# A chunk's attention scores as one product per head, with the level-by-level path kept behind a branch

## The chip, the cores and the metric

The kernel runs on one core of one Trainium2 chip. Its engines work side by side and meet at semaphores: TensorE (PE; its weight loads are listed apart as PEld), VectorE (DVE), ScalarE (ACT), GpSimd (POOL) and SyncE (SP). TensorE takes its operands from SBUF and leaves its results in PSUM, from where DVE or ACT fetch them. In this kernel SP and ACT issue the DMAs. The metric is the time of one execution on the device in microseconds; the less, the better.

## The reference

An RWKV-5 attention block (4 batches, 8 heads, 768 tokens, 48 channels a head) is followed by a feed-forward block with a softmax linear unit (3072 tokens, 384 to 1024 to 384):

```python
for t in range(S):
    kt, vt, rt = (k[:, :, t], v[:, :, t], r[:, :, t])
    cur = np.einsum('bhd,bhe->bhde', u[None] * kt, vt)
    y[:, :, t] = np.einsum('bhd,bhde->bhe', rt, state + cur)
    state = w[None, :, :, None] * state + np.einsum('bhd,bhe->bhde', kt, vt)
...
h = x @ w_in
e = np.exp(h - np.max(h, axis=-1, keepdims=True))
solu = h * (e / (np.sum(e, axis=-1, keepdims=True) + 1e-09))
mu, var = solu.mean(-1, keepdims=True), solu.var(-1, keepdims=True)
ln = (solu - mu) / np.sqrt(var + 1e-06) * g_ln
return ln @ w_out
```

The inputs are random. w, the decay of each channel, lies between 0.85 and 0.95. The two weight matrices arrive as float64; all arithmetic is float32.

## The kernel before

**Units.** The 768 tokens of a batch are cut into 6 chunks of 128 tokens. A unit is one chunk of one batch; there are 24, chunk by chunk with the four batches inside, so that a batch's next chunk comes four units after the one whose state it needs.

**Scores.** Inside a chunk, token s reaches a later token t with the weight w^(t-1-s). The kernel splits the 128 by 128 triangle into seven levels L = 64, 32, ..., 1: a pair (s, t) belongs to the level whose block of 2L tokens has s in its lower half and t in its upper half. For each level but the last, `prepare` multiplies the transposed k on POOL (L231) and the transposed r on DVE (L233) with powers of w whose exponents are never negative; the results are the tiles `z`. `scores` multiplies the halves on TensorE, 8 heads a level (L266), and brings them from PSUM into the score matrix `AT`: levels 64 and 32 by copies on ACT (L279), the other five by predicated copies on DVE (L274). `AT` is set to zero once, at the start. The token itself, weighted by u, goes another way: `rku` = k * u * r on POOL (L245, L246), its sum `own` per head on DVE (L248), and `yd` = v * own on POOL (L250), which is added to y.

**y and the state.** `finish` computes y = rs @ state + AT @ v on TensorE (L290, L295), where `rs` is r times powers of w (DVE, L237), adds `yd` on DVE (L299), and updates the state: k times powers (`kp`, POOL, L240) with v on TensorE (L304), the old state times w^128 on POOL (L307), the sum on DVE (L313).

**Feed-forward.** `ffn_in` transposes x, multiplies with w_in (`h_ps`, L328), and then runs a chain in which each step needs the one before: maximum of h (DVE, L332), exp with its sum (ACT, L334), one over the sum (DVE, L336), the product `solu` with its sum (DVE, L338), the square with its sum (ACT, L342), the variance and its power -1/2 (POOL, L343 and L345), the normalisation of `solu` (DVE, L346). `ffn_out` transposes the result (`t_ps`, L357), copies it out of PSUM (`lnT`, half on DVE and half on ACT), and multiplies with w_out (`o_ps`, L364).

**The loop.** Pass i loads unit i+2, prepares unit i+1, and writes `ffn_in(i-3)`, `scores(i)`, `ffn_out(i-3)`, `finish(i)` in this order. In the first three passes the float64 weights are turned into float32, 14 pieces with seven DVE operations and one or two POOL operations each (L128 to L145). A scheduler then orders the instructions of each engine. Within an engine that order is fixed. Operands carry the buffer's number where the rows further down show one.

Of the kernel before, what the change touches and what calls it, by code (L numbers as in the profile page):

```python
# [9 lines left out]
F32 = mybir.dt.float32  # L10
U32 = mybir.dt.uint32
ACT = mybir.ActivationFunctionType
ALU = mybir.AluOpType
AX = mybir.AxisListType
PSUM = bass.MemoryType.PSUM


@with_exitstack
def kernel(
    ctx: ExitStack,  # L20
    tc: tile.TileContext,
    r: bass.AP,
# [6 lines left out]
    moe_g_ln: bass.AP,  # L29
    out: bass.AP,  # L30
):
    """The recurrence runs in chunks of T = 128 tokens.  Within a chunk token s reaches a later
    token t with the weight w^(t-1-s).  The pair belongs to the one level L (64, 32, ..., 1) whose
    blocks of 2L tokens have s in the lower and t in the upper half; with m the first token of the
    upper half, w^(t-1-s) = w^(t-m) * w^(m-1-s), and neither exponent is ever negative: no w can
    make a factor overflow or be divided by.  A state carries the tokens of the chunks before.

    moe_w_in and moe_w_out come as the words of float64 and are rounded to float32 here; the
    arithmetic is float32 throughout."""
    nc = tc.nc  # L40
    B, H, S, D = r.shape
    T = 128
    P = 64
    C = S // T
    HP = H // 2
    dm = H * D
    dff = moe_w_in.shape[1]
    KD = dm // 128
    KF = dff // 128
    NX = 512  # L50
    LAG = 3
# [3 lines left out]
    const = ctx.enter_context(tc.tile_pool(name="const", bufs=1))  # L55
    apool = ctx.enter_context(tc.tile_pool(name="apool", bufs=2))
    zpool = ctx.enter_context(tc.tile_pool(name="zpool", bufs=2))
    fpool = ctx.enter_context(tc.tile_pool(name="fpool", bufs=2))
    wpool = ctx.enter_context(tc.tile_pool(name="wpool", bufs=2))
    small = ctx.enter_context(tc.tile_pool(name="small", bufs=4))  # L60
    psA = ctx.enter_context(tc.tile_pool(name="psA", bufs=3, space=PSUM))
    psH = ctx.enter_context(tc.tile_pool(name="psH", bufs=1, space=PSUM))
    psM = ctx.enter_context(tc.tile_pool(name="psM", bufs=3, space=PSUM))

    ctx.enter_context(nc.allow_non_contiguous_dma(reason="rows of w and g to the partitions"))

    # chunk-major, so that a batch's next chunk comes B units after the one it waits for
    units = [(b, c) for c in range(C) for b in range(B)]

# [1 line left out]
    NLD = 4  # L71
    rpads = [const.tile([128, H, P], F32, name=f"rpad{i}") for i in range(NLD)]
    kpads = [const.tile([128, H, P], F32, name=f"kpad{i}") for i in range(NLD)]
# [8 lines left out]
            nc.sync.dma_start(out=t[i % NLD][:, :, 0:D],  # L82
                              in_=src[b, :, ts(c, T), :].rearrange("h s d -> s h d"))

# [1 line left out]
    wd = const.tile([128, HP, 1], F32, name="wd")  # L86
    u_bc = const.tile([128, H, D], F32, name="u_bc")
    g_sb = const.tile([128, KF], F32, name="g_sb")
# [9 lines left out]
    load(1)  # L98
    nc.scalar.dma_start(out=g_sb, in_=moe_g_ln.rearrange("(c p) -> p c", p=128))

# [1 line left out]
    def words(x):  # L102
        n, m = x.shape
        t = bass.DRamTensorHandle(x.tensor.name, (n, 2 * m), U32)
# [13 lines left out]
    def convert(j):  # L118
        dst, _, f = pieces[j]
        n = dst.shape[1]  # L120
        raw = raws.pop(j)
        lo, hi = raw[:, :, 0], raw[:, :, 1]
        bias = (1023 - 127) << 20
        ex = wpool.tile([128, n], U32, tag="ex", name="ex")
        ma = wpool.tile([128, n], U32, tag="ma", name="ma")
        low = wpool.tile([128, n], F32, tag="low", name="low")
        # the sign and the exponent, 0 when it lies below float32's: +-2^e
        nc.vector.tensor_single_scalar(out=ex, in_=hi, scalar=0x7FF00000, op=ALU.bitwise_and)  # L128
        nc.vector.tensor_scalar(out=ex, in0=ex, scalar1=float(bias),
                                scalar2=float(bias + (255 << 20)), op0=ALU.max, op1=ALU.min)  # L130
        nc.vector.tensor_scalar(out=ex, in0=ex, scalar1=float(bias), scalar2=8.0,
                                op0=ALU.subtract, op1=ALU.mult)
        nc.vector.scalar_tensor_tensor(out=ex, in0=hi, scalar=0x80000000, in1=ex,
                                       op0=ALU.bitwise_and, op1=ALU.bitwise_or)
        # with the first 20 bits of the fraction, and what the other 32 add
        nc.vector.tensor_scalar(out=ma, in0=hi, scalar1=3, scalar2=0x007FFFF8,
                                op0=ALU.logical_shift_left, op1=ALU.bitwise_and)
        nc.vector.tensor_tensor(out=ma, in0=ma, in1=ex, op=ALU.bitwise_or)
        nc.vector.scalar_tensor_tensor(out=low, in0=lo, scalar=2.0 ** -52, in1=ex.bitcast(F32),
                                       op0=ALU.mult, op1=ALU.mult)  # L140
        if f is None:
            nc.gpsimd.tensor_add(dst, ma.bitcast(F32), low)
        else:
            nc.gpsimd.tensor_add(low, ma.bitcast(F32), low)
            nc.gpsimd.tensor_scalar(out=dst, in0=low, scalar1=g_sb[:, f : f + 1], scalar2=1.0,  # L145
                                    op0=ALU.mult, op1=ALU.mult)
# [6 lines left out]
    neg_half = const.tile([128, 1], F32, name="neg_half")  # L153
    nc.vector.memset(neg_half, -0.5)

    # tab[.., n] = w^n and rev[.., n] = w^(T-1-n), channels on the partitions (two heads a column)
    tab = const.tile([128, HP, T], F32, name="tab")
    rev = const.tile([128, HP, T], F32, name="rev")
    pw = const.tile([128, 8, HP, 1], F32, name="pw")
# [7 lines left out]
        nc.vector.tensor_mul(rev[:, :, T - 2 * n : T - n], rev[:, :, T - n : T], step)  # L167
        nc.vector.tensor_mul(pw[:, j + 1], pw[:, j], pw[:, j])

    # w^(T-1-s) with the tokens on the partitions  # L170
    kdec = const.tile([128, HP, 128], F32, name="kdec")
    kd_ps = psM.tile([128, HP, 128], F32, tag="m", name="kd_ps")
    for a in range(HP):
        nc.tensor.transpose(kd_ps[:, a, :], rev[:, a, :], ident)
    nc.vector.tensor_copy(out=kdec, in_=kd_ps)

    # masks[L][s, j, n] = token s lies in the lower half of the j-th block of 2L
    masks = {}
    for L in MASKED:
        nb = 64 // L  # L180
# [7 lines left out]
        nc.vector.tensor_copy(out=mi[:, 0, :], in_=mf.rearrange("p j n -> p (j n)"))  # L188
        masks[L] = mi

    # AT[s, h, t]: only s < t is ever written, the rest stays zero
    NAT = 2
    ATs = [const.tile([128, H, T], F32, name=f"AT{i}") for i in range(NAT)]
    for t in ATs:
        nc.gpsimd.memset(t, 0.0)
    # the state of each batch, two heads to a block diagonal
    states = [const.tile([128, HP, 2, D], F32, name=f"state{b}") for b in range(B)]
    for t in states:
        nc.vector.memset(t, 0.0)
# [7 lines left out]
        x = t.rearrange("p a (j o n) -> p a j o n", o=2, n=L)  # L207
        return x[:, :, :, 0, :], x[:, :, :, 1, :]

# [1 line left out]
    def prepare(i):  # L211
        b, c = units[i]
        kt, rt, vt = kpads[i % NLD], rpads[i % NLD], vts[i % NLD]
        X = live[i] = {}
        kT = apool.tile([128, HP, T], F32, name="kT")
        rT = apool.tile([128, HP, T], F32, name="rT")
        for src, dst in ((kt, kT), (rt, rT)):
            ps = psM.tile([128, HP, T], F32, tag="m", name="tr_ps")
            for a in range(HP):
                nc.tensor.transpose(ps[:, a, :], pair(src, a), ident)  # L220
            nc.scalar.copy(out=dst, in_=ps)  # L221
        X["kT"], X["rT"] = kT, rT
        X["z"] = {}
        for ls in LEVELS:
            for L in ls:
                if L == 1:
                    continue
                z = X["z"][L] = zpool.tile([128, HP, T], F32, name=f"z{L}")
                shape = [128, HP, 64 // L, L]
                (k_lo, _), (_, r_up), (z_lo, z_up) = halves(kT, L), halves(rT, L), halves(z, L)  # L230
                nc.gpsimd.tensor_mul(z_lo, k_lo,  # L231
                                     rev[:, :, T - L : T].unsqueeze(2).to_broadcast(shape))
                nc.vector.tensor_mul(z_up, r_up,  # L233
                                     tab[:, :, 0:L].unsqueeze(2).to_broadcast(shape))
        if c > 0:
            X["rs"] = apool.tile([128, HP, T], F32, name="rs")
            nc.vector.tensor_mul(X["rs"], rT, tab)  # L237
        if c < C - 1:
            X["kp"] = apool.tile([128, H, P], F32, name="kp")
            nc.gpsimd.tensor_mul(X["kp"].rearrange("p h d -> p (h d)"),  # L240
                                 kt.rearrange("p h d -> p (h d)"),
                                 kdec.rearrange("p a d -> p (a d)"))
        # the token itself, weighted by u
        rku = apool.tile([128, H, D], F32, name="rku")
        nc.gpsimd.tensor_mul(rku, kt[:, :, 0:D], u_bc)  # L245
        nc.gpsimd.tensor_mul(rku, rku, rt[:, :, 0:D])  # L246
        own = small.tile([128, H, 1], F32, name="own")
        nc.vector.tensor_reduce(out=own[:, :, 0], in_=rku, axis=AX.X, op=ALU.add)  # L248
        X["yd"] = apool.tile([128, H, D], F32, name="yd")
        nc.gpsimd.tensor_mul(X["yd"], vt, own.to_broadcast([128, H, D]))  # L250

# [1 line left out]
    def scores(i):  # L253
        X = live[i]
        AT = X["AT"] = ATs[i % NAT]
# [22 lines left out]
                            rows = slice(2 * L * j, 2 * L * j + L)  # L278
                            nc.scalar.copy(out=dst[rows, :, j, :], in_=src[rows, :, j, :])  # L279

# [1 line left out]
    def finish(i):  # L282
        b, c = units[i]
        X = live[i]
# [29 lines left out]
                else:  # L314
                    nc.vector.tensor_copy(out=St[rows, :, q, :], in_=kv_ps[rows, :, q, :])

# [1 line left out]
    def ffn_in(i):  # L318
        X = live[i]
        xt_ps = psM.tile([128, KD, 128], F32, tag="m", name="xt_ps")  # L320
# [25 lines left out]
        nc.vector.tensor_scalar(out=solu, in0=solu, scalar1=nmu, scalar2=rstd,  # L346
                                op0=ALU.add, op1=ALU.mult)

# [1 line left out]
    def ffn_out(i):  # L350
        b, c = units[i]
        X = live.pop(i)
# [40 lines left out]
            finish(i)  # L393


# [1 line left out]
_INS = ['r', 'k', 'v', 'w', 'u', 'moe_w_in', 'moe_w_out', 'moe_g_ln']  # L397
_OUTS = [((3072, 384), 'float32')]
# [25 lines left out]
```

## Time and profile before

| What | Value |
|---|---|
| Time, median of 3 runs | 907.26 us (906.92 to 908.93) |
| The profiled execution: its span | 905.3 us, 1.96 below that median |
| TensorE busy | 784.0 us (87% of the span) |
| its weight loads | 601.0 us (66%) |
| DVE busy | 448.1 us (49%) |
| ACT busy | 158.8 us (18%) |
| POOL busy | 285.0 us (31%) |
| Score matmuls L266, busy together | 341.5 us (272.6 + 68.9) |

The span runs from the first to the last instruction; the timed runs hold a little more than it. A matmul in float32 shows as two records, a transpose as one. Matmuls are pipelined, so the busy time of TensorE is a share of the span in which some matmul was under way, not a measure of how full the array was. "Idle before" with an arrow names the operation whose end let the engine go on.

### The profile page before, as it was taken

Reading aid. Unit: us, or ns where it says so; the run is one execution under the profiler, and the core shown is the slowest. Engines: PE = TensorE matmul, PEld = TensorE weight load, DVE = VectorE, ACT = ScalarE, POOL = GpSimd, SP = SyncE. Lnnn points to the kernel's source line nnn. Section 1 sums busy time; section 2 is a strip of 40 time slices with the busy share of each in tenths; the row PEclk is TensorE's granted clock in tenths of the full one; section 3 lists DMA queues with packets and bytes.
Section 4 is the critical chain, followed back from the end, with each engine's and each line's share of the span. In section 5 each row is a group of like instructions: output and inputs, shape, how many; then the busy total and the mean of one; then the engine's idle time right before and its main releaser. Section 6 shows DMA issues by size and latency. Waiting matters only on the chain.

```text
span 905.3 us, 11284 instructions
## 1 busy us (share of the span) xinstructions
PE 784.0 (87%) x4524; PEld 601.0 (66%) x4524; DVE 448.1 (49%) x826; ACT 158.8 (18%) x361; POOL 285.0 (31%) x345
## 2 busy tenths in 40 slices
PE   1564979999999999999999999999999999998665
PEld 1553977677677677677677677777777677766332
DVE  6969767336346346346346346346346435613111
ACT  1101102121121121121121121121122122111111
POOL 5937544404404404404314314314313212200000
PEclk9555557868868868868868868868869876887877
DMA  9413101101101101101101101101100000000000
GB/s 244 79 53 79 27 1 27 35 1 36 35 1 35 36 1 36 35 1 35 35 1 36 35 1 35 35 1 36 35 1 18 18 10 1 10 9 9 9 9 9
DMA packets 82003, 26.09 MB, mean 29 GB/s; under 512 B 76960, under 2 KB 80160, under 8 KB 81952
## 3 DMA queue, kind: packets, MB, share of 16 engines
q1 hardware_dynamic: 78336, 18.88, 10.1%
q10 hardware_dynamic: 3616, 6.49, 2.4%
q8 instruction: 36, 0.59, 0.2%
q14 instruction: 15, 0.12, 0.0%
HBM read 20.65 MB, written 4.72 MB: 28 GB/s over the span
## 4 chain that ended last, share of the span: by engine, by line
PE 64%; POOL 15%; DVE 15%; issue 2%; DMA 2%; ACT 1%; POOLq 0%; ACTq 0%; DVEq 0%
PE at L266 24%; PE o_ps L364 19%; POOL z L231 7%; PE h_ps L328 6%; PE y_ps L295 5%; PE t_ps L357 5%; DVE AT L274 3%; DVE st L332 2%; POOL rku L245 2%; DVE z L233 2%; PE y_ps L290 2%; POOL kp L240 2%; POOL rku L246 2%; POOL yd L250 1%; PE kv_ps L304 1%
## 5 line engine op out<-in xcount | busy, mean ns | idle before, releaser
L266 PE MATMUL at<-z 48*128 48x64 f32 (+1 forms) x2304 | 272.6, 336 | 67.7 <-DVE AT L274 58.7
L266 PEld LDWEIGHTS at<-z 48*128 48x128 f32 (+1 forms) x2304 | 252.4, 242 | 103.7 <-issue 90.3
L364 PE MATMUL o_ps<-w_out_sb,lnT 128*128 128x384 f32 x384 | 175.4, 624 | 0.0
L364 PEld LDWEIGHTS o_ps<-w_out_sb,lnT 128*128 128x128 f32 x384 | 93.7, 252 | 70.6 <-issue 40.6
L299 DVE TENSOR_TENSOR x<-y_ps,yd 128x384 f32<-128x384 f32 x24 | 13.4, 557 | 243.9 <-PE y_ps L295 243.9
L274 DVE COPY_PREDICATED AT<-mask,at 128x256 f32<-128x256 uint32 x240 | 120.2, 549 | 23.9 <-PE at L266 21.5
L328 PE MATMUL h_ps<-w_in_sb,xT 128*128 128x512 f32 x288 | 130.0, 601 | 1.9 <-ACT xT L324 1.8
L233 DVE TENSOR_TENSOR z<-rT,tab 128x256 f32<-128x256 f32 x144 | 114.0, 856 | 17.9 <-ACT rT L221 17.9
L231 POOL TENSOR_TENSOR z<-kT,rev 128x256 f32<-128x256 f32 x144 | 119.8, 863 | 1.2 <-ACT kT L221 1.2
L328 PEld LDWEIGHTS h_ps<-w_in_sb,xT 128*128 128x128 f32 x288 | 52.7, 190 | 61.5 <-issue 57.4
L343 POOL TENSOR_SCALAR st<-st 128x1 f32<-128x1 f32 x24 | 4.6, 190 | 256.3 <-ACT sq L342 256.3
L307 POOL TENSOR_TENSOR state<-state,pw 128x384 f32<-128x384 f32 x16 | 13.2, 826 | 218.9 <-PE y_ps L290 218.9
L266 PE MATMUL at<-rT,kT 48*128 48x64 f32 x384 | 68.9, 405 | 1.0 <-DVE AT L274 1.0
L357 PE MATMUL t_ps<-ident,solu 128*128 128x128 f32 x192 | 47.1, 427 | 25.3 <-DVE solu L346 25.3
L266 PEld LDWEIGHTS at<-rT,kT 48*128 48x128 f32 x384 | 64.1, 310 | 1.5 <-PE at L266 1.5
L334 ACT ACTIVATE e<-h_ps,st 128x1024 f32<-128x1024 f32 x24 | 26.7, 1114 | 190.6 <-DVE st L332 190.6
L357 PEld LDWEIGHTS t_ps<-ident,solu 128*128 128x128 f32 x192 | 37.6, 223 | 30.3 <-issue 17.0
L279 ACT COPY AT<-at 64x256 f32<-64x256 f32 (+1 forms) x144 | 37.4, 292 | 84.4 <-PE at L266 83.1
L295 PE MATMUL y_ps<-vt,AT 128*128 128x48 f32 x384 | 51.4, 290 | 0.0
L295 PEld LDWEIGHTS y_ps<-vt,AT 128*128 128x128 f32 x384 | 50.1, 209 | 0.6
L332 DVE TENSOR_REDUCE st<-h_ps 128x1 f32<-128x1024 f32 x24 | 29.4, 1224 | 41.1 <-PE h_ps L328 40.6
L359 DVE COPY lnT<-t_ps 128x512 f32<-128x512 f32 x24 | 16.6, 691 | 57.7 <-PE t_ps L357 57.7
(69 smaller groups left out, 611.3 us busy)
## 6 DMA issues: line engine op xcount, KB each, us to landing
kpad<-in_k_dram SPq DMA_DIRECT2D x24, 192.0 KB, 3.3
rpad<-in_r_dram SPq DMA_DIRECT2D x24, 192.0 KB, 3.8
vt<-in_v_dram SPq DMA_DIRECT2D x24, 192.0 KB, 2.6
out_dram<-o SPq DMA_DIRECT2D x24, 192.0 KB, 1.9
raw<-in_moe_w_in_dram ACTq DMA_DIRECT2D x6, 512.0 KB, 6.4
raw<-in_moe_w_out_dram ACTq DMA_DIRECT2D x8, 384.0 KB, 3.1
u_bc<-in_u_dram ACTq DMA_DIRECT2D x1, 192.0 KB, 4.1
wd<-in_w_dram ACTq DMA_DIRECT2D x2, 0.8 KB, 7.2
```

Of the source, the lines that this page charges most:

```text
L231: nc.gpsimd.tensor_mul(z_lo, k_lo, rev[:, :, T - L : T].unsqueeze(2).to_broadcast(shape))
L233: nc.vector.tensor_mul(z_up, r_up, tab[:, :, 0:L].unsqueeze(2).to_broadcast(shape))
L240: nc.gpsimd.tensor_mul(X["kp"].rearrange("p h d -> p (h d)"), kt.rearrange("p h d -> p (h d)"), kdec.rearrange("p a d -> p (a d)"))
L266: nc.tensor.matmul(pss[q][0:M, n, a, :], lo[rows, a, 0:M], rhs, start=True, stop=True)
L274: nc.vector.copy_predicated(dst, m.to_broadcast([128, HP, 64 // L, L]), src)
L279: nc.scalar.copy(out=dst[rows, :, j, :], in_=src[rows, :, j, :])
L295: nc.tensor.matmul(y_ps[:, h, :], AT[:, h, :], vt[:, h, :], start=first, stop=(h == H - 1), skip_group_check=True)
L328: nc.tensor.matmul(h_ps[:, ts(n, NX)], xT[:, j, :], w_in_sb[:, j, ts(n, NX)], start=(j == 0), stop=(j == KD - 1))
L332: nc.vector.tensor_reduce(out=nmax, in_=h_ps, axis=AX.X, op=ALU.max, negate=True)
L334: nc.scalar.activation(out=e, in_=h_ps, func=ACT.Exp, bias=nmax, accum_out=se)
L357: nc.tensor.transpose(t_ps[:, f, :], X["solu"][:, ts(4 * g + f, 128)], ident)
L364: nc.tensor.matmul(o_ps, lnT[:, f, :], w_out_sb[:, f, :], start=(f == 0), stop=(f == KF - 1))
```

## The change

The new kernel has two paths. `general_path` is the kernel above, word for word. `direct_path` is new and runs always; at its end, if any decay lies outside 0.75 to 1.25, `general_path` runs as well and overwrites the output.

In `direct_path` the weight w^(t-1-s) is written as w^(127-s) * w^-(128-t). k with the first factor is `kp`, which was already needed for the state; r with the second one, `fore`, is the new `rT` (DVE, straight out of the transpose's PSUM). One matmul per head (128 columns) gives all scores of a chunk; two predicated copies of 128x512 bring the part above the diagonal into `AT`. POOL writes the diagonal (`own`) and zeros into `AT` ahead of them, so `yd`, the zeroed `AT`, the `z` tiles, `rs`, and six of seven levels' masks are gone. x comes out of PSUM by a copy on ACT. The state carries a factor w^128 in advance, multiplied in on POOL. PSUM holds 2 score buffers of double width instead of 3 and 4 others instead of 3.

```diff
-    psA = ctx.enter_context(tc.tile_pool(name="psA", bufs=3, space=PSUM))
-    psM = ctx.enter_context(tc.tile_pool(name="psM", bufs=3, space=PSUM))
+    psA = ctx.enter_context(tc.tile_pool(name="psA", bufs=2, space=PSUM))
+    psM = ctx.enter_context(tc.tile_pool(name="psM", bufs=4, space=PSUM))
...
+    nc.vector.tensor_mul(fore, back, pw[:, 0].to_broadcast([128, HP, T]))
+    nc.vector.reciprocal(out=fore, in_=fore)
...
     def prepare(i):
+        X["kp"] = kp = apool.tile([128, H, P], F32, name="kp")
+        nc.gpsimd.tensor_mul(kp.rearrange("p h d -> p (h d)"),
+                             kt.rearrange("p h d -> p (h d)"),
+                             kdec.rearrange("p a d -> p (a d)"))
...
+        AT = X["AT"] = apool.tile([128, H, T], F32, name="AT")
+        nc.gpsimd.tensor_mul(AT, ident.unsqueeze(1).to_broadcast([128, H, T]),
+                             own.to_broadcast([128, H, T]))
...
+        for a in range(HP):
+            nc.tensor.transpose(ps[:, a, :], pair(rt, a), ident)
+        nc.vector.tensor_mul(X["rT"], ps, fore)
...
+            nc.tensor.transpose(ps[:, a, :], pair(kp, a), ident)
+        nc.scalar.copy(out=X["kT"], in_=ps)
...
     def scores(i):
+        for a in range(HP):
+            for q in range(2):
+                rows = slice(q * P, q * P + D)
+                nc.tensor.matmul(pss[q][:, a, :], X["kT"][rows, a, :], X["rT"][rows, a, :],
+                                 start=True, stop=True)
+        for q in range(2):
+            nc.vector.copy_predicated(A4[:, :, q, :], later.to_broadcast([128, HP, T]), pss[q])
...
     def finish(i):
-        nc.vector.tensor_add(x, y_ps.rearrange("p h d -> p (h d)"),
-                             X["yd"].rearrange("p h d -> p (h d)"))
+        nc.scalar.copy(out=x, in_=y_ps.rearrange("p h d -> p (h d)"))
...
+                nc.vector.tensor_add(St, kv_ps, St)
+                nc.gpsimd.tensor_mul(St, St, wt)
...
+def tile_rwkv5_eagle__then__act_solu_kernel(tc: tile.TileContext, *args):
+    with tc.tile_pool(name="flag", bufs=1) as pool:
+        bad = direct_path(tc, pool, *args)
+        value = tc.nc.values_load(bad, min_val=0, max_val=1)
+        with tc.If(value != 0):
+            general_path(tc, *args)
```

How the order moves, at three places of the middle of the run. First TensorE, from the product with w_in on. Before, 22 rows with 46 score matmuls of two units stand between h_ps and t_ps, these among them:

```order
L328 MATMUL h_ps<-w_in_sb,xT 128x512 x6
...
L266 MATMUL at_1776<-z_1485 128x64 x4
L266 MATMUL at_1776<-z_1488 128x64 x4
L266 MATMUL at_1777<-z_1485 128x64 x4
L266 MATMUL at_1777<-z_1488 128x64 x4
L266 MATMUL at_1798<-rT,kT 128x64 x4
L266 MATMUL at_1799<-rT,kT 128x64 x4
L266 MATMUL at_1931<-z_1674 64x64 x4
L266 MATMUL at_1932<-z_1674 64x64 x4
...
L357 MATMUL t_ps<-ident,solu 128x128 x8
```

Now, with the rows ahead of h_ps too (tr_ps are the transposes of r, tk_ps those of kp):

```order
L652 MATMUL kv_ps<-vt_91,kp 128x96 x4
L610 MATMUL tr_ps<-ident,rpad_85 128x128 x4
L614 MATMUL tk_ps<-ident,kp 128x128 x4
L665 MATMUL xt_ps<-ident,x 128x128 x3
L625 MATMUL at_1499<-rT,kT 128x128
L625 MATMUL at_1500<-rT,kT 128x128
L671 MATMUL h_ps<-w_in_sb,xT 128x512 x6
...
L700 MATMUL t_ps<-ident,solu 128x128 x8
L707 MATMUL o_ps<-w_out_sb,lnT 128x384 x8
L639 MATMUL y_ps<-state_187,rT 128x96 x4
```

The line left out stands for six more matmuls of L625. Between h_ps and t_ps stand 6 score matmuls where there were 46.

Second POOL, around the power that ends the statistics of one unit (L345 before, L688 now; st is the small tile of statistics). Before, its next work is the state and yd:

```order
L343 TENSOR_SCALAR st_1716<-st_1716 128x1
L345 TENSOR_TENSOR st_1716<-st_1716,neg_half_135 128x1
L307 TENSOR_TENSOR state3_208<-state3_208,pw_139 128x384
L250 TENSOR_TENSOR yd_1902<-vt1_91,own_1900 128x384
L240 TENSOR_TENSOR kp_1895<-kpad1_87,kdec_164 128x512
```

Now:

```order
L686 TENSOR_SCALAR st_1709<-st_1709 128x1
L688 TENSOR_TENSOR st_1709<-st_1709,neg_half_137 128x1
L604 TENSOR_TENSOR AT_1792<-ident_132,own_1790 128x1024
L595 TENSOR_TENSOR kp_1785<-kpad3_89,kdec_160 128x512
L656 TENSOR_TENSOR state1_186<-state1_186,wt_181 128x384
L599 TENSOR_TENSOR rku_2235<-kpad3_89,u_bc_103 128x384
```

The diagonal (L604) and kp moved directly behind the power; before, the next operation there waited for TensorE's y.

Third DVE, from the sums of the state to the copy of the transposed result. Before (between these two pieces stand six z products):

```order
L313 TENSOR_TENSOR state3_208<-kv_ps_1850,state3_208 64x4x48 x2
...
L237 TENSOR_TENSOR rs_1893<-rT_1862,tab_137 128x512
L248 TENSOR_REDUCE own_2704<-rku_2701 128x8
L332 TENSOR_REDUCE st_1917<-h_ps_1910 128x1
L274 COPY_PREDICATED AT0_201<-mask16_175,at0_1955 128x4x4x16
```

Now:

```order
L655 TENSOR_TENSOR state0_185<-kv_ps_1663,state0_185 128x384
L611 TENSOR_TENSOR rT_1683<-tr_ps_1684,fore_140 128x512
L602 TENSOR_REDUCE own_2126<-rku_2123 128x8
L675 TENSOR_REDUCE st_1709<-h_ps_1702 128x1
L628 COPY_PREDICATED AT_1680<-later_167,at0_1835 128x4x128
L628 COPY_PREDICATED AT_1680<-later_167,at1_1836 128x4x128
L678 TENSOR_SCALAR st_1709<-st_1709 128x1
L679 RECIPROCAL st_1709<-st_1709 128x1
L681 SCALAR_TENSOR_TENSOR solu_1715,st_1709<-h_ps_1702,st_1709,e_1711 128x1024
L683 TENSOR_SCALAR st_1709<-st_1709 128x1
L689 TENSOR_SCALAR solu_1715<-solu_1715,st_1709 128x1024
L702 COPY lnT_1735<-t_ps_1736 128x512
```

The z products are gone, rT stands in the place of the state's rs, and both predicated copies of a unit stand together between the maximum and the steps that need exp.

271 lines of the change are left out of this document (270 added, 1 removed).

## The prediction

> **What bounds the kernel now.** I read the chain of waits on the page first, then the chain and TensorE's timeline through one unit in the middle of the run, then the tail. The page's chain, by engine:
>
> ```profile
> PE 64%; POOL 15%; DVE 15%; issue 2%; DMA 2%; ACT 1%; POOLq 0%; ACTq 0%; DVEq 0%
> ```
>
> Only 64% of the chain that ended last is on TensorE, though it is the busiest engine; 15% is on POOL and 15% on DVE. So TensorE's work alone does not set the period. The chain through one unit shows where it leaves TensorE, right behind y (columns: start, duration, what):
>
> ```profile
> 410.87 0.83 POOL yd L250
> 411.70 1.23 POOL kp L240
> 412.93 4.02 POOL z L231 x5
> ```
>
> It runs over POOL (yd, kp, the z products, then two rku products), goes back to DVE (own, then the maximum of h), and only then to the score matmuls of L266. TensorE in the same unit:
>
> ```profile
> 400.58 7.00 PE L364 MATMUL o_ps<-w_out_sb,lnT 128*128 128x384 f32 x16
> 407.43 1.03 PE L290 MATMUL y_ps<-state,rs 128*128 128x96 f32 x8
> 408.29 1.91 PE L295 MATMUL y_ps<-vt,AT 128*128 128x48 f32 x16
> 410.04 1.10 PE L304 MATMUL kv_ps<-vt,kp 128*128 128x96 f32 x8
> 410.97 0.60 PE L220 MATMUL tr_ps<-ident,kpad 128*128 128x128 f32 x4
> ...
> 413.38 5.42 PE L328 MATMUL h_ps<-w_in_sb,xT 128*128 128x512 f32 x12
> 418.72 2.67 PE L266 MATMUL at<-z 48*128 48x64 f32 x28
> ...
> 431.45 1.97 PE L357 MATMUL t_ps<-ident,solu 128*128 128x128 f32 x8
> ...
> 434.40 7.16 PE L364 MATMUL o_ps<-w_out_sb,lnT 128*128 128x384 f32 x16
> ```
>
> One unit takes 434.40 - 400.58 = 33.8 us. From the start of h_ps (413.38) to the transposes t_ps of the normalised result (431.45) pass 18.1 us: 5.3 for h_ps itself and 12.7 in which score matmuls run, while the maximum, exp, product, square and normalisation of h go over DVE, ACT and POOL. In the tail the last units have no scores left, and that chain stands alone:
>
> ```profile
> 848.73 6.51 PE L364 MATMUL o_ps<-w_out_sb,lnT 128*128 128x384 f32 x16
> ...
> 856.19 5.42 PE L328 MATMUL h_ps<-w_in_sb,xT 128*128 128x512 f32 x12 [0.62 <-ACT xT L324]
> 861.64 1.22 DVE L332 TENSOR_REDUCE st<-h_ps 128x1 f32<-128x1024 f32 x1 [12.97 <-PE h_ps L328]
> 862.96 1.11 ACT L334 ACTIVATE e<-h_ps,st 128x1024 f32<-128x1024 f32 x1 [6.83 <-DVE st L332]
> ...
> 868.34 0.81 DVE L346 TENSOR_SCALAR solu<-solu,st 128x1024 f32<-128x1024 f32 x1 [2.28 <-POOL st L345]
> 869.30 1.94 PE L357 MATMUL t_ps<-ident,solu 128*128 128x128 f32 x8 [7.70 <-DVE solu L346]
> ...
> 871.17 7.23 PE L364 MATMUL o_ps<-w_out_sb,lnT 128*128 128x384 f32 x16
> ...
> 894.34 7.59 PE L364 MATMUL o_ps<-w_out_sb,lnT 128*128 128x384 f32 x16
> ```
>
> From h_ps to t_ps: 869.30 - 856.19 = 13.1 us, 7.7 of them with TensorE empty. This floor stays when the scores go, and the change does not touch it.
>
> **The change, part by part.** All terms go against the profiled execution, whose span is 905.3 us; the median of the timed runs is 907.3, so 2.0 is added at the end for what lies around the span.
>
> *Scores.* 56 matmuls a unit with 64 columns become 8 with 128; in the new order 2 stand ahead of h_ps and 6 behind it. Those 6 need no price: even if each of their 12 records took twice the 95 ns of the 28 records at 418.72, they would end within 2.3 us, far inside the 7.7. So the 12.7 us between h_ps and t_ps shrink towards 7.7, and TensorE waits in them. The six z products on POOL and the six on DVE, the six ACT copies and eight of the ten predicated copies go, and with them the chain's detour over POOL.
>
> *What the chain gets instead, first:* two predicated copies of 128x512 on DVE between the maximum and 1/sum. Four of 128x256 back to back took:
>
> ```profile
> 121.77 1.42 DVE L274 COPY_PREDICATED AT<-mask,at 128x256 f32<-128x256 uint32 x4
> ```
>
> Two of double width should take as long, 1.4 us, while ACT computes exp (1.11 at 862.96, and the reading of its sum). They delay the chain by 0 to 0.3; I take 0.2. At the mean of all 240 old copies (0.549, row further down) it would be 0.9.
>
> *Second, and larger:* POOL writes the diagonal into AT, 128x1024, right behind the power that ends the statistics, just when DVE wants to normalise solu. Do the two get in each other's way? Rows of DVE and POOL at work at once:
>
> ```profile
> 46.51 4.74 POOL L142 TENSOR_TENSOR w_in_sb<-ma,low 128x512 f32<-128x512 f32 x2 [2.84 <-DVE low L139]
> 50.06 1.47 DVE L136 TENSOR_SCALAR ma<-raw 128x512 uint32<-128x512 uint32 x1 [1.16 <-POOL w_in_sb L142]
> 118.58 0.35 DVE L131 TENSOR_SCALAR ex<-ex 128x384 uint32<-128x384 uint32 x1
> 118.74 1.04 POOL L144 TENSOR_TENSOR low<-ma,low 128x384 f32<-128x384 f32 x1 [1.96 <-DVE low L139]
> 118.85 1.15 DVE L136 TENSOR_SCALAR ma<-raw 128x384 uint32<-128x384 uint32 x1
> ```
>
> A TENSOR_SCALAR takes 0.35 us with POOL quiet (118.58). At 118.85 one starts under a POOL product and takes 1.15, ending 0.22 after that product: it waited for the whole of it. The first pair is the very case: POOL has two products in a row, the end of the first releases DVE at 50.06, the second is already on, and DVE takes 1.47, again until 0.28 after POOL's end. So I expect the diagonal to come first and the normalisation to wait. The trace has no such diagonal; yd (0.83 at 410.87) has the same form, one operand repeated, for 384 elements, so 1024 take 2.2. After it the waiting operation still needs its length less 0.13 (0.35 - 0.22): 0.81 - 0.13, about 0.65. The normalisation ends 2.2 + 0.65 instead of 0.81 after the power: **+2.0 us**. Bounds: 0 if DVE gets there first, 2.3 at the rate of kp (1.23 for 512). It hits 19 of the 24 units; in the order the last five have no diagonal behind their power.
>
> *Between o_ps and h_ps:* y and kv stay, so kv ends 10.4 to 10.5 us after o_ps starts (410.97 - 400.58). The transposes of k and r become those of r and kp, as many; ACT copies kT and xT in the slots in which it copied rT and xT, so h_ps starts 2.4 later as before (413.38 - 410.97). DVE has the state sum and rT there, both short. POOL has rku, which needs the new kpad:
>
> ```profile
> kpad<-in_k_dram SPq DMA_DIRECT2D x24, 192.0 KB, 3.3
> ```
>
> That load waits for kv now. It lands some 4 us after kv, the two rku products and own end at about 6.5, and the maximum of h needs DVE at 7.8 (2.4 + 5.4): hidden, with 1 us to spare. A later load would show at once.
>
> So a full period is 10.5 + 2.4 + 13.1 + 0.2 + 2.0 + 1.9 (t_ps to o_ps in the tail) = **30.1 us** against 33.8.
>
> *The start.* When h_ps and o_ps run first, and the copies:
>
> ```profile
> L328 PE MATMUL h_ps<-w_in_sb,xT x288: 592/592/697, 139.4 to 884.2; 128*128 128x512 f32 x144
> L364 PE MATMUL o_ps<-w_out_sb,lnT x384: 486/486/1009, 160.2 to 901.4; 128*128 128x384 f32 x192
> L274 DVE COPY_PREDICATED AT<-mask,at 128x256 f32<-128x256 uint32 x240 | 120.2, 549 | 23.9 <-PE at L266 21.5
> ```
>
> The first h_ps starts at 139.4, the first o_ps at 160.2. Until then DVE and POOL take turns, as above, at converting 14 pieces of weights and at their other work, so what is taken off either shortens the stretch. Off: 29 z products, run in alternation on both, 29 x 0.8 (4.02 for five) = 23; 30 copies of 0.55 become 6 of 0.7, 12; masks, the second power table and three sums, about 7; TensorE's long scores ahead of y, about 3. On: five diagonals for four yd, 7.5; four rT on DVE, a product and a reciprocal for the new table, 4 (the trace has a reciprocal of one column only; at several times a product it would be 7). In sum 34 less, which puts the first h_ps at 105; bounds are 90, with TensorE's waits gone too, and 120, with half of the removal covered. From there 13.1 + 0.2 + 2.0 + 1.9, and 1.8 for the cold start and two more copies, lead to the first o_ps at 124.
>
> *The sum.* The first period has no state part (0.9, 407.43 to 408.29) and takes 29.2; 16 full ones 481.6; one without kv 29.2; one without kv and diagonal 27.2. Two with y alone are taken from the tail, from this row to the one at 848.73:
>
> ```profile
> 822.72 7.56 PE L364 MATMUL o_ps<-w_out_sb,lnT 128*128 128x384 f32 x16
> ```
>
> 2 x 26.0; then 22.4 (848.73 to 871.17) and 23.2; from the last o_ps (894.34) to the end of the span 11.0. Together 124 + 29.2 + 481.6 + 29.2 + 27.2 + 52.0 + 45.6 + 11.0 = 799.8.
>
> *The branch.* The test of w is a handful of small DVE instructions at the start, in the wait for the first weights. At the end every engine loads one word and jumps over the old path. No row has such a load or jump. The nearest is a DMA, 3.3 us for kpad's 192 KB; a word should not take longer. I take 1.9 and keep 0 and 6.6 (two such trips). [...] Span 801.7, time **803 us** after rounding.
>
> **The rivals.** *DVE gets there first.* POOL's diagonal and DVE's normalisation are let go by the same end, and hundredths of a microsecond decide. For it: DVE stands ready, with nothing else to do. Against it: the pair at 50.06. Then 19 x 2.0 us go: 765.
>
> *A longer chain.* Copies at their mean price (+0.7), the diagonal at kp's rate (+0.3), the load of kpad late (+0.6): with all of them 1.6 in 19 units, 833.
>
> *The clock, and slower than before.* TensorE stands still for some 8 to 10 us in each unit. If it came back at half speed and stayed so, h_ps would take 5.3 us more and o_ps perhaps half of its 7 more: +8.8 in 18 periods, 961. From 5.5 us a period on, the gain is eaten (104 us over 19 units). Against it: in the tail TensorE stands for 7.7 us as well, and h_ps still takes 5.42 and o_ps 6.51 to 7.59, against 5.42, 7.00 and 7.16 in the middle.
> [...]
>
> *The branch is taken.* w lies between 0.85 and 0.95 and the limits are 0.75 and 1.25, so the old path should not run. If it did, both would, and the time would be about 1,700 us.
>
> **How the numbers follow.** Chances: the forecast (803) 0.60, DVE first (765) 0.22, a longer chain (833) 0.13, the clock 0.04, the branch taken 0.01. The range from 758 to 835 holds the first three, on the low side with an early start too. A difference under 0.2% can't be told from none. Faster 0.95; within 0.2% 0.01, out of the clock's 0.04; slower 0.04.
>
> **What would show it.** In the profile after: o_ps every 30.1 us; normalisations of about 2.8 us that end some 0.65 behind POOL's diagonal, and of 0.8 in the last five units; TensorE waiting for solu ahead of t_ps; the first h_ps near 105. A normalisation of 0.8 everywhere means the first rival, an h_ps longer than 5.4 the third, score rows of the old path the last. The forecast falls if the wait ahead of t_ps is far from 10 us, or if another engine, POOL above all, holds up the start of h_ps.

## The result, and the profile after

| | Before | After |
|---|---|---|
| Time, median | 908.1 us of 4 runs (906.92 to 909.56) | 824.17 us of 4 runs (823.54 to 825.66) |
| Ratio | | 0.9077, 95% interval 0.9061 to 0.9093 |
| Span of the profiled execution | 905.3 us | 822.7 us |
| TensorE busy | 784.0 us | 548.8 us (67%) |
| DVE, ACT, POOL busy | 448.1, 158.8, 285.0 us | 249.9, 121.2, 184.3 us |
| h_ps, 288 records, busy | 130.0 us | 169.1 us |
| First h_ps, first o_ps | 139.4, 160.2 us | 100.0, 115.3 us |

The forecast was 803 us, with a range from 758 to 835. The time lies in the range, 21 above the forecast (the span of 801.7 and the 2.0 around it make 803.7, which the prediction writes as 803). But the unit in the middle of the run is not the one that was forecast. First the page's chain by engine, then a unit of TensorE's timeline and the start of the next (start, duration, in brackets the idle time ahead and what ended it):

```profile
PE 60%; DVE 18%; POOL 8%; ACT 8%; issue 4%; DMA 1%; ACTq 0%; POOLq 0%
```

```profile
437.32 7.47 PE L707 MATMUL o_ps<-w_out_sb,lnT 128*128 128x384 f32 x16
...
447.24 1.10 PE L652 MATMUL kv_ps<-vt,kp 128*128 128x96 f32 x8
448.17 0.60 PE L610 MATMUL tr_ps<-ident,rpad 128*128 128x128 f32 x4
450.65 0.66 PE L614 MATMUL tk_ps<-ident,kp 128*128 128x128 f32 x4 [1.88 <-POOL kp L595]
...
452.71 8.29 PE L671 MATMUL h_ps<-w_in_sb,xT 128*128 128x512 f32 x12
460.94 0.94 PE L625 MATMUL at<-rT,kT 48*128 48x128 f32 x12
468.71 1.94 PE L700 MATMUL t_ps<-ident,solu 128*128 128x128 f32 x8 [6.83 <-DVE solu L689]
470.58 6.21 PE L707 MATMUL o_ps<-w_out_sb,lnT 128*128 128x384 f32 x16
```

This unit takes 470.58 - 437.32 = 33.3 us, and the one ahead of it 31.6; the two alternate, 32.4 on average where 30.1 was forecast. Two things are new. TensorE stands for 1.88 us ahead of tk_ps, until POOL has written kp (39.8 us in the whole run, by the group of tk_ps). And h_ps takes 8.29 us (7.43 in the unit ahead) where it took 5.42 before. POOL and DVE in the unit ahead, where y_ps runs from 412.64 and kv_ps from 414.38, say where kp comes from:

```profile
402.31 0.55 POOL L688 TENSOR_TENSOR st<-st,neg_half 128x1 f32<-128x1 f32 x1
414.63 1.90 POOL L604 TENSOR_TENSOR AT<-ident,own 128x1024 f32<-128x1024 f32 x1 [11.77 <-PE y_ps L644]
416.49 1.26 POOL L595 TENSOR_TENSOR kp<-kpad,kdec 128x512 f32<-128x512 f32 x1
```

```profile
402.90 0.81 DVE L689 TENSOR_SCALAR solu<-solu,st 128x1024 f32<-128x1024 f32 x1 [2.28 <-POOL st L688]
```

The diagonal does not run behind the power (402.31). POOL stands for 11.77 us and starts it when y_ps is through; kp comes behind it and ends at 417.75, and the transposes of kp start at 417.80. The normalisation L689 meets no product of POOL and takes 0.81, in the other units as well (812 ns on average over the 24).

TensorE's granted clock in that unit, the one ahead of it (h_ps starts at 420.32) (columns: stretch, length, busy time with records, clock, DMA share, GB/s):

```profile
core 0: us, PE busy (x), PEclk, DMA share, GB/s
415.90:417.80 1.90, 0.02 (x1) 0.94 0.55 104
417.80:420.32 2.52, 2.48 (x11) 0.50 0.57 114
420.32:424.30 3.98, 3.98 (x7) 0.50 0.17 26
424.30:427.68 3.38, 3.38 (x8) 0.98 0.00 0
```

In the hole (415.90 to 417.80) the clock stands at 1.00 but for the very end, then falls to 0.50 and stays there until about 424.4, some 4 us into h_ps.

### The profile page after: what moved, and what is told of

Its sections match the earlier page's. It is cut to its first block, busy times and chain, and to the rows that moved or that the text cites. A ratio compares the mean times of both kernels' runs of the same rounds, so it can differ in the third digit from the quotient of the medians.

```text
span 822.7 us, 5801 instructions
## 1 busy us (share of the span) xinstructions
PE 548.8 (67%) x2220; PEld 351.4 (43%) x2220; DVE 249.9 (30%) x441; ACT 121.2 (15%) x217; POOL 184.3 (22%) x193
## 4 chain that ended last, share of the span: by engine, by line
PE 60%; DVE 18%; POOL 8%; ACT 8%; issue 4%; DMA 1%; ACTq 0%; POOLq 0%
PE h_ps L671 20%; PE o_ps L707 20%; PE y_ps L644 6%; PE t_ps L700 6%; DVE solu L681 4%; POOL AT L604 4%; ACT sq L685 4%; DVE st L675 4%; ACT e L677 4%; POOL kp L595 3%; DVE solu L689 2%; PE tk_ps L614 2%; PE y_ps L639 2%; PE at L625 2%; POOL st L688 2%
## 5 line engine op out<-in xcount | busy, mean ns | idle before, releaser
L671 PE MATMUL h_ps<-w_in_sb,xT 128*128 128x512 f32 x288 | 169.1, 749 | 2.5 <-ACT xT L667 2.5
L671 PEld LDWEIGHTS h_ps<-w_in_sb,xT 128*128 128x128 f32 x288 | 67.8, 244 | 89.0 <-issue 83.4
L604 POOL TENSOR_TENSOR AT<-ident,own 128x1024 f32<-128x1024 f32 x24 | 45.7, 1903 | 238.9 <-PE y_ps L644 236.6
L614 PE MATMUL tk_ps<-ident,kp 128*128 128x128 f32 x96 | 21.4, 363 | 39.8 <-POOL kp L595 39.8
L625 PE MATMUL at<-rT,kT 48*128 48x128 f32 x384 | 42.3, 347 | 5.4 <-ACT kT L615 3.8
L625 PEld LDWEIGHTS at<-rT,kT 48*128 48x128 f32 x384 | 31.6, 227 | 28.3 <-issue 16.8
L689 DVE TENSOR_SCALAR solu<-solu,st 128x1024 f32<-128x1024 f32 x24 | 19.5, 812 | 54.1 <-POOL st L688 54.1
L599 POOL TENSOR_TENSOR rku<-kpad,u_bc 128x384 f32<-128x384 f32 x24 | 24.4, 1016 | 46.5 <-DMA kpad<-in_k_dram 46.5
L685 ACT ACTIVATE sq<-solu,st 128x1024 f32<-128x1024 f32 x24 | 27.5, 1147 | 48.3 <-DVE st L683 48.3
L710 ACT COPY o<-o_ps 128x384 f32<-128x384 f32 x24 | 11.5, 479 | 149.3 <-PE o_ps L707 149.3
L614 PEld LDWEIGHTS tk_ps<-ident,kp 128*128 128x128 f32 x96 | 14.5, 184 | 44.3 <-POOL kp L595 44.3
```

Of the source, the lines that this page charges most:

```text
L604: nc.gpsimd.tensor_mul(AT, ident.unsqueeze(1).to_broadcast([128, H, T]), own.to_broadcast([128, H, T]))
L614: nc.tensor.transpose(ps[:, a, :], pair(kp, a), ident)
L625: nc.tensor.matmul(pss[q][:, a, :], X["kT"][rows, a, :], X["rT"][rows, a, :], start=True, stop=True)
L671: nc.tensor.matmul(h_ps[:, ts(n, NX)], xT[:, j, :], w_in_sb[:, j, ts(n, NX)], start=(j == 0), stop=(j == KD - 1))
L685: nc.scalar.activation(out=sq, in_=solu, func=ACT.Square, bias=nmu, accum_out=ss)
```

## The experiments

Each edit is made in the changed kernel; the times stand beside 908 to 909 us of the kernel before on the same chip.

**A third buffer for kp.**

```diff
-        X["kp"] = kp = apool.tile([128, H, P], F32, name="kp")
+        X["kp"] = kp = apool.tile([128, H, P], F32, name="kp", bufs=3)
```

> kp gets a third buffer, so that POOL writes it one unit earlier and the transposes tk_ps no longer stand behind the diagonal. My theory: the hole of 1.88 us ahead of tk_ps goes, and with it the half clock: TensorE's clock falls around 417.6 because of that hole, and h_ps (7.43 or 8.29 us) then begins cold. So h_ps comes back to 5.42, kv end to h_ps from 4.8 to some 2.2, and a full period from 32.4 (31.6 and 33.3 in turn) to 27.5: 16 periods x 4.9 = 78, span near 741. Rival A: the half clock ahead of h_ps comes from the narrow matmuls and transposes there, not from the hole: h_ps stays at 7.4 to 8.3, only the hole and the cold transposes go (2.4 us), span near 784. Rival B: the transposes wait for something else that is late next (the diagonal's y, the copy of kT): the hole stays in another place, span near 820.

Measured: 744.65 us (743.09 to 745.19), ratio 0.8189 (0.8165 to 0.8213), span 742.8. A unit of TensorE's timeline:

```profile
389.44 6.80 PE L707 MATMUL o_ps<-w_out_sb,lnT 128*128 128x384 f32 x16
...
399.63 0.60 PE L610 MATMUL tr_ps<-ident,rpad 128*128 128x128 f32 x4
400.07 0.60 PE L614 MATMUL tk_ps<-ident,kp 128*128 128x128 f32 x4
...
401.76 5.42 PE L671 MATMUL h_ps<-w_in_sb,xT 128*128 128x512 f32 x12
...
416.75 6.80 PE L707 MATMUL o_ps<-w_out_sb,lnT 128*128 128x384 f32 x16
```

The hole is gone, h_ps takes 5.42 in every unit (130.0 us in all), and the period is 27.3. One buffer of 2 KB per partition is worth 80 us. POOL still writes the diagonal behind y_ps and kp behind it, but this kp is needed one unit later. Rivals A (span 784) and B (span 820) fall.

**TensorE busy in the hole, kp as late as before.**

```diff
-        for a in range(HP):
-            nc.tensor.transpose(ps[:, a, :], pair(rt, a), ident)
+        for _ in range(4):
+            for a in range(HP):
+                nc.tensor.transpose(ps[:, a, :], pair(rt, a), ident)
```

> The four transposes of r are done four times over, with the same result, so that TensorE has about 1.8 us more to do just where it waits for kp; kp itself comes as late as before. My theory (the hole makes the clock fall): the wait ahead of tk_ps shrinks to under 0.3, the clock stays at 1.0, h_ps takes 5.42 in all units, and the period falls by 2.44 (h_ps) and about 0.3 (the other cold ones) to 29.7: span near 779, although TensorE got more work. Rival A (the narrow work in that stretch makes it fall): h_ps stays at 7.4 to 8.3, span 822 or a little more. Rival B (kp's wait alone costs, the clock is a by-product of something else): the same as A.

Measured: 786.83 us (785.07 to 787.6), span 783.3.

```profile
453.33 1.91 PE L611 MATMUL tr_ps<-ident,rpad 128*128 128x128 f32 x16
455.83 0.66 PE L615 MATMUL tk_ps<-ident,kp 128*128 128x128 f32 x4 [0.58 <-POOL kp L595]
...
457.58 5.42 PE L672 MATMUL h_ps<-w_in_sb,xT 128*128 128x512 f32 x12
```

Line 611 is the transposes of r here, 672 is h_ps. Twelve more transposes a unit, kp no earlier, and the kernel is 37 us faster: h_ps is back at 5.42 throughout, and in the unit shown the granted clock stays at 1.00 from 453.33 to 463.00, so that both rivals (a span of 822 or more) fall. The hole costs twice, once as a wait and once through the clock. Here the wait stays (from tr_ps to h_ps still pass 4.2 us) and the second price is gone; with the third buffer both are gone, which is 42 us more.

**A product of POOL behind the power.**

```diff
+        extra = fpool.tile([128, H, T], F32, name="extra", bufs=1)
+        nc.gpsimd.tensor_mul(extra, ident.unsqueeze(1).to_broadcast([128, H, T]),
+                             rstd.unsqueeze(2).to_broadcast([128, H, T]))
         nc.vector.tensor_scalar(out=solu, in0=solu, scalar1=nmu, scalar2=rstd,
```

> A POOL product of the diagonal's shape (128x1024, one operand repeated) into a tile that nobody reads is put directly behind the power in every unit: the case that my prediction charged with 2.0 us. My theory: POOL comes first, DVE's normalisation takes 2.7 to 2.8 instead of 0.81 and ends some 0.65 behind POOL's product; 24 x 2.0 = 48 longer, span near 870. Rival: DVE comes first, the normalisation stays at 0.81 and the span at 823, with POOL's product the one that is delayed.

Measured: 845.51 us (844.15 to 845.88), span 843.5. The normalisation has line 692 here, the added product 690:

```profile
440.96 2.48 DVE L692 TENSOR_SCALAR solu<-solu,st 128x1024 f32<-128x1024 f32 x1 [2.28 <-POOL st L688]
```

```profile
441.00 1.89 POOL L690 TENSOR_TENSOR extra<-ident,st 128x1024 f32<-128x1024 f32 x1
```

The normalisation takes 2.48 in all 24 units and ends 0.55 behind the product. DVE's record even starts first, by 0.04, and is still through only behind it. So the wait that the prediction charged exists: beside a product of 1.89 the normalisation loses 1.67 (2.0 was forecast). In the changed kernel, where it takes 0.81, it just has no occasion. The span grew by only 21 and not by 24 x 1.67 = 40, mostly because h_ps got shorter (151.9 us in all instead of 169.1, 17 of the 19 us that are missing; 6.0 to 7.5 in a unit with the hole, where the changed kernel has 7.4 to 8.3). That with another period the half clock covers another part of h_ps is an estimate from these lengths.

**A third buffer for AT.**

```diff
-        AT = X["AT"] = apool.tile([128, H, T], F32, name="AT")
+        AT = X["AT"] = apool.tile([128, H, T], F32, name="AT", bufs=3)
```

> AT alone gets a third buffer (kp keeps two). The order of POOL then writes the diagonal of one unit further ahead, at the same place, and it waits for TensorE again, for the y of the unit three back. My theory: since the work runs ahead as far as the buffers allow, the new wait is met by the same y_ps; the diagonal stays behind it, kp behind the diagonal, the hole at 1.88 and the span at 822. Rival: with a buffer more the diagonal is free at the power; then the normalisation is blocked (2.5 us as in the run with a product there, 0.81 otherwise) while kp follows right behind kv and the hole shrinks to 0.8 or less: span under 800.

Measured: 823.92 us (821.68 to 825.0), no change. The groups of the diagonal and of tk_ps:

```profile
L604 POOL TENSOR_TENSOR AT<-ident,own 128x1024 f32<-128x1024 f32 x24 | 45.8, 1909 | 224.8 <-PE y_ps L644 222.5 <-DVE own L602 2.3
L614 PE MATMUL tk_ps<-ident,kp 128*128 128x128 f32 x96 | 21.4, 363 | 38.9 <-POOL kp L595 38.9
```

The diagonal waits for y_ps as before (222.5 us in all), and TensorE for kp. With the new buffer the scheduler writes the diagonal one unit further ahead, at the same place, and running ahead as far as its buffers reach it waits for the newest reader again.

**Fillers in the gap ahead of t_ps.** The gap of 6.8 us halves the clock as well, at the expense of t_ps and o_ps: in the changed kernel it falls to 0.50 at 431.23, in the gap from 428.62 to 435.45, and stays there until 441.47, through t_ps and the first 4.2 us of o_ps. With kp in three buffers:

```diff
         nc.vector.tensor_reduce(out=nmax, in_=h_ps, axis=AX.X, op=ALU.max, negate=True)
+        warm = psM.tile([128, NX], F32, tag="m", name="warm")
+        for _ in range(1):
+            nc.tensor.matmul(warm[0:1, :], nmax, w_in_sb[:, 0, 0:NX], start=True, stop=True)
         e = fpool.tile([128, dff], F32, name="e")
         nc.scalar.activation(out=e, in_=h_ps, func=ACT.Exp, bias=nmax, accum_out=se)
+        for _ in range(5):
+            nc.tensor.matmul(warm, e[:, 0:128], w_in_sb[:, 0, 0:NX], start=True, stop=True)
```

> kp with three buffers, and six matmuls whose result nobody reads fill the gap of 6.8 us between the last score matmul and t_ps: one of one row as soon as the maximum is there, five of 128x512 as soon as exp is. Theory (the gap lets TensorE's clock fall, as the hole did): the clock stays up, t_ps takes about 1.2 instead of 1.94 and o_ps about 5.5 instead of 6.80, the period falls from 27.3 to about 25.3 and the span to about 695. Rival: what is left of the gap (about 1 us ahead of the five, 0.5 behind) still halves the clock, t_ps and o_ps stay as they are, span 743, or more where the fillers at half clock end behind the normalisation.

> As the run before, without the filler behind the maximum, so that about 1.8 us stay empty between the last score matmul and the five fillers: as long as the hole of 1.88 us that halved the clock ahead of h_ps. Theory, if any hole of that length inside otherwise full work halves the clock: no gain, span 740 or more. Rival: it depends on where the hole falls in the clock's own rhythm, so that some units gain: between 700 and 740. If the clock stays up all the same: near 695.

Measured with six: 699.57 us (698.59 to 699.85), ratio 0.7699 (0.7678 to 0.772), span 698.0, and 699.66 in the five runs of the repetition. Part of a unit, and the clock on the page:

```profile
412.69 0.94 PE L625 MATMUL at<-rT,kT 48*128 48x128 f32 x12
414.07 1.02 PE L678 MATMUL warm<-w_in_sb,st 128*1 128x512 f32 x2 [0.45 <-DVE st L675]
415.37 4.56 PE L682 MATMUL warm<-w_in_sb,e 128*128 128x512 f32 x10 [0.28 <-ACT e L680]
420.46 1.06 PE L705 MATMUL t_ps<-ident,solu 128*128 128x128 f32 x8 [0.53 <-DVE solu L694]
421.87 5.43 PE L712 MATMUL o_ps<-w_out_sb,lnT 128*128 128x384 f32 x16 [0.35 <-DVE lnT L707]
```

```profile
PEclk9999999999999999999999999999999999999999
```

t_ps takes 1.06 instead of 1.94, o_ps 5.43 instead of 6.80, the period is 25.5. In the other runs of this kernel the mean clock is 0.95 to 1.00 and the time the same: in the trace of the repetition (0.952) it stands at 0.50 from 38.3 to 103.1 us, until just behind the start of the first h_ps (102.4), and at 1.00 from there to 680. This version does useless work and beats both kernels. With five fillers, the hole of 1.75 ahead of them left, 707.1 us (705.91 to 709.37), between 700 and 740 as the rival had it. There the same hole does harm in one unit and none in the next (a unit at 442 and the next at 469):

```profile
442.40 0.94 PE L625 MATMUL at<-rT,kT 48*128 48x128 f32 x12
445.08 6.25 PE L682 MATMUL warm<-w_in_sb,e 128*128 128x512 f32 x10 [1.75 <-ACT e L680]
...
468.85 0.94 PE L625 MATMUL at<-rT,kT 48*128 48x128 f32 x12
471.53 4.56 PE L682 MATMUL warm<-w_in_sb,e 128*128 128x512 f32 x10 [1.75 <-ACT e L680]
```

**Fillers alone,** six of them, kp with two buffers.

> The six fillers in the changed kernel as it is, kp with two buffers: the gap ahead of t_ps is filled, the hole of 1.88 us ahead of tk_ps stays. Theory (a hole of that length halves the clock even where TensorE works all the time otherwise): t_ps about 1.1 and o_ps 5.43, but h_ps still 7 to 8: period 25.5 + 1.9 + 0.4 + 2.4 = 30.2, 16 x 2.2 and the tail's gain of some 15 below 822, span near 770. Rival (the hole halves the clock only because the gap of 6.8 us has done so shortly before): h_ps 5.42, period 27.8, span near 733.

Measured: 755.38 us (753.53 to 758.16), span 755.2. The hole and h_ps of one unit:

```profile
417.93 0.66 PE L614 MATMUL tk_ps<-ident,kp 128*128 128x128 f32 x4 [1.88 <-POOL kp L595]
...
419.68 7.12 PE L671 MATMUL h_ps<-w_in_sb,xT 128*128 128x512 f32 x12
```

The hole alone does slow TensorE: h_ps takes 149.8 us in all, 5.9 to 7.6 in the units with the hole, against 130.0 without, and the mean clock is 0.918, against 0.952 in the repetition with three buffers for kp (both pages show half the clock in some slices ahead of the first h_ps). That it is less than 7 to 8 each time puts the span 15 under the theory's 770; on when the clock falls the last section has measurements.

**The branch.** Left out in three kernels (the changed one, the one with three buffers for kp, the one with six fillers): the old path and the branch to it. The last of the four runs is the kernel with six fillers, branch and all, once more.

```diff
-        value = tc.nc.values_load(bad, min_val=0, max_val=1)
-        with tc.If(value != 0):
-            general_path(tc, *args)
```

> The old path and the branch in front of it are left out; the flag is still computed. Theory: the branch costs what the end of the span grew by beyond the last copy out, 4.9 us from there to the end against 2.9 before the change, so 2.0: span 820.7, time 822.2. Rival: the end grew for another reason (the write of the output): 0, time 824.2. Second rival: the branch costs more than the end shows (the code of the old path delays the start as well): 4 or more.

> kp with three buffers and without the old path and its branch, against the run with three buffers alone (744.65, runs from 743.1 to 745.2; 5 us from the last copy out to the end). Theory: the branch costs 1.9 at the end of the span and nothing else: median 742.7. Rival: the time around the span takes it back, median 744.6.

> Three buffers for kp, six fillers, and no old path with its branch. With the clock at 1.0 throughout, the runs of the kernel with fillers lie within 1.3 us, so that a difference of 1.9 can be told, which the pairs before could not. Theory: the branch costs 1.9 at the end and nothing is given back: 1.9 below the run beside it. Rival: no difference, as in both pairs before.

> The kernel with three buffers for kp and six fillers once more, beside the run without the branch: 699.6 expected, within 1.0, and the interval against the kernel before from more rounds.

The last copy out of PSUM (L710) ends at 817.83 (817.35 + 0.48) in the changed kernel and at 817.78 (817.30 + 0.48) without the branch. From its end to the end of the span pass 4.9 us with the branch (822.7) and 3.0 without (820.8). So the branch puts 1.9 at the end. The medians show less of it: 824.17 and 824.13 in the changed kernel, 744.65 and 744.49 with three buffers, 699.66 (699.28 to 700.59) and 698.9 (698.53 to 700.22) with fillers. What takes it back ahead of the last copy isn't settled. The pair with three buffers was measured on two chips (909.4 and 908.1 us for the kernel before); the last pair, on one chip, differs by 0.8 with ranges that overlap. So the time that the branch costs lies between 0 and 1.9.

## Why the prediction was right, and where it was not

The range held the time and the sign was right, but the middle came near by terms that cancel. That is luck in part: without the 38 us for a diagonal that runs elsewhere the forecast would have been its first rival's 765, 59 below what was measured. And one of the signs by which the prediction itself says that it falls is there: POOL holds up the start of h_ps. The other, a wait ahead of t_ps far from 10 us, is met in part, with some 7. The sum, by its own steps, against the span of 822.7 (801.7 forecast):

| Step | Forecast | Measured | Difference |
|---|---|---|---|
| first o_ps | 124 | 115.3 | -8.7 |
| first period | 29.2 | 31.1 | +1.9 |
| 15 full periods | 15 x 30.1 | 15 x 32.4 (485.5) | +34.0 |
| the next three | 86.5 | 81.7 | -4.8 |
| four of the tail | 97.6 | 96.7 | -0.9 |
| the end, with the branch | 12.9 | 12.4 | -0.5 |

*The scores and the floor of the chain.* Right. TensorE waits for solu ahead of t_ps in every unit (6.8 us, and 0.94 of score matmuls beside it), and from the end of h_ps to t_ps pass 7.7, the tail's value of before.

*The two copies,* 0.2. They take 1.31 together from 428.93, and the step towards 1/sum starts at 430.35, when ACT has read the sum of exp (430.31): nothing, within the bounds given.

*The diagonal behind the power,* +2.0 in 19 units, 38 in all: it failed. "POOL writes the diagonal into AT, 128x1024, right behind the power" was read from the order, in which the two stand side by side. But AT has two buffers, and the diagonal must wait for the y that reads the older one. (The row at 118.58 was misread, too: POOL isn't quiet there but starts a product at 118.74, and the DVE operation that was already on took its 0.35 all the same.) The wait itself is real and was priced nearly right; the run with the added product shows it (1.67). It came out as the rival "DVE gets there first", by another cause: there was no race.

*"h_ps starts 2.4 later as before",* behind kv: it failed. 4.5 to 5.0 were measured. ACT's slots, DVE and rku were weighed, and rku with own was hidden as forecast; but the transposes of kp need kp itself, and kp stands behind the diagonal, 1.90 + 1.26 behind y_ps. The diagonal is not all of it: kp has two buffers too, and kv_ps, which ends at 415.48 (414.38 + 1.10), reads the older one. Without the diagonal kp could have started then instead of at 416.49, so by an estimate from these rows 1.0 of the 1.88 us is the diagonal's and 0.9 would have stayed; no run moved the diagonal alone. Before, kp was needed by kv_ps only. The order in the section on the change shows both, kp behind the diagonal on POOL and tk_ps<-kp on TensorE.

*h_ps at 5.42:* it failed, by 2.4 a unit. The clock was a rival with the right sign ("an h_ps longer than 5.4"), priced at 8.8 a period and given 0.04, because h_ps runs at full speed in the tail in spite of a gap of 7.7. That row doesn't bear on it: o_ps lies between that gap and the next h_ps, and the clock comes back under it (1.00 from 850.95 to 854.36, h_ps at 856.19). What counted in the changed kernel is a hole just ahead of h_ps (1.88 us), and the trace of before already had the like, 2 us among score matmuls, with a clock of 0.55 behind it:

```profile
418.70:421.40 2.70, 2.69 (x29) 1.00 0.00 0
421.40:424.00 2.60, 0.62 (x6) 1.00 0.00 0
424.00:427.00 3.00, 3.00 (x26) 0.55 0.02 5
```

There it lies behind h_ps, so the half clock fell on other work. So the failed terms per full period are -2.0 for the diagonal, -0.2 for the copies, -0.3 from o_ps to kv, +2.4 for the wait and +2.4 for the clock: +2.3, as measured (32.4 - 30.1).

*The start,* first h_ps at 105: 100.0. It was mis-sized, as was the way from there to the first o_ps (15.4 instead of 19: 13.5 to t_ps and 1.9 to o_ps, so neither the 2.2 of the diagonal and the copies nor most of the 1.8 for a cold start, which no row showed, can be seen: the first h_ps takes 5.49 and its t_ps 1.97). DVE up to the first h_ps, before and after (the columns are PE, PEld, DVE, ACT and POOL busy):

```profile
0.00:139.40 139.40, 80.92 (x482) 76.57 (x482) 108.39 (x215) 12.21 (x30) 83.96 (x97) 0.61 0.36 81
```

```profile
0.00:100.00 100.00, 34.21 (x176) 30.92 (x176) 85.83 (x154) 6.13 (x10) 59.20 (x59) 0.69 0.51 114
```

DVE has 22.6 less work (108.39 to 85.83) and 16.8 less idle time. The forecast took 34 off, all as work; waits were only in its lower bound. Which of them went by which edit wasn't tried.

*The branch,* 1.9 with bounds of 0 and 6.6: no run had shown such a load or jump. Measured are 1.9 at the end, 0 to 1.9 in the time.

## What to carry to other kernels

Rows that stand side by side in an engine's order need not be neighbours in time (here the power ended at 402.86 and the diagonal started at 414.63): for each instruction that is moved, ask which buffer it writes and who last reads it, and then what stands behind it on its engine. A producer's extra buffer paid where the waiting reader needed that very tile: the third buffer for kp gave 80 us, that for AT nothing. And TensorE, with less to do (busy for 548.8 us where it was 784.0), ran h_ps slower (169.1 us where it was 130.0): look at the granted clock stretch by stretch, also in the kernel before, for holes just ahead of the large matmuls.

## What the hardware showed beyond that

In the traces of both kernels the granted clock changes on a grid of 3.41 us. In the changed kernel it is mixed in these half microseconds (same columns as above):

```profile
407.00:407.50 0.50, 0.50 (x2) 0.66 0.00 0
417.50:418.00 0.50, 0.20 (x1) 0.58 0.24 47
424.00:424.50 0.50, 0.50 (x2) 0.60 0.00 0
431.00:431.50 0.50, 0.00 (x0) 0.73 0.00 0
441.00:441.50 0.50, 0.50 (x2) 0.53 0.00 0
451.50:452.00 0.50, 0.15 (x4) 0.71 0.63 108
```

From the share of 0.50 in each, the changes lie at 407.34, 417.58, 424.40, 431.23, 441.47 and 451.71, that is 3, 2, 2, 3 and 3 times 3.41 us apart. Read in the same way over the whole trace, all 83 changes (38.70 to 820.35) lie on this grid within 0.01 us, and the 52 of the kernel before (24.92 to 898.73) lie on one of the same step. Cut the trace at the grid into windows of 3.41 us. The clock fell behind windows in which the records show TensorE busy for 1.75 (414.17 to 417.58), 1.45 (448.30 to 451.71) and, with five fillers, 1.66 of 3.41 us, and stayed up behind one with 1.96, where the same hole of 1.75 lay across two windows. So with five fillers the hole of 1.75 us cost or not according to where it fell.

But the busy time in the records doesn't decide alone. With five fillers the clock fell behind one window with 1.66 us and stayed up behind another with 1.67; in the kernel before it fell behind a window that was busy throughout:

```profile
493.98:497.39 3.41, 1.66 (x14) 1.00 0.00 0
497.39:500.81 3.42, 3.42 (x5) 0.50 0.00 0
521.29:524.70 3.41, 1.67 (x11) 1.00 0.00 0
524.70:528.11 3.41, 3.31 (x8) 1.00 0.00 0
```

```profile
383.32:386.73 3.41, 3.41 (x30) 1.00 0.00 0
386.73:390.15 3.42, 1.43 (x8) 0.50 0.00 0
```

What else counts no run here shows. The units of 31.6 and 33.3 us in turn fit the same grid: their sum, 64.85, is 19 such windows.
